# A long convolution with an expert block behind it, on one core: both transposes of a token tile in one place, half of a product on another engine, two loads exchanged, and two stages spread over more chunks

## The chip, the cores and the metric

The kernel runs on one core of a Trainium2 chip. A core has TensorE (PE in the profile; its weight loads are shown apart as PEld), VectorE (DVE), ScalarE (ACT), GpSimd (POOL) and SyncE (SP), which issues all of this kernel's DMAs. The metric is the device time of one execution in microseconds. Each engine works through its own instructions in the order in which the program has them.

## The reference

Two blocks follow each other. The first is a long convolution along the sequence, for a batch B of 4, a sequence S of 12480 and a model width D of 128:

```python
h = np.maximum(pos_emb @ w1, 0.0) @ w2          # S x D filter
h = h * np.exp(-0.01 * np.arange(S))[:, None]
u = x * v                                       # B x S x D
y = causal convolution of u with h along S      # by FFTs of length 2 S
z = x * y
```

The second takes the B * S = 49920 rows of z as tokens, with d_ff = 2048:

```python
h = z @ w_in
out = (h * np.cos(h)) @ w_out                   # 49920 x 128
```

All values are float32, two inputs (the expert's weights) come as float64.

## The kernel before

**The convolution.** The sequence is cut as 120 columns (n2) of 104 rows, and the transform of length 2 * 96 * 120 is done in two steps of small matrix products each way. A batch passes through four stages, each a generator that puts out a little work at a time: F1 (`f1_units`, 64 units), the first forward step; F2 (`f2_units`, 48 units), the second, whose results DVE multiplies with the filter's spectrum (L479, L481) and POOL adds (L482); I1 (`i1_units`, 64 units), the first inverse step, evicted by ACT and DVE (L494, L496); and I2 (`i2_units`, 30 groups of 4 columns), the second inverse step. A group of I2 needs a table `tm` of 312 KB, made or loaded from DRAM (`td`), and the 208 KB of x that belong to it (`xs`); DVE multiplies the matmuls' result by x in place (L518), and SP stores that as z in DRAM (`zd`). While a batch is in I2, x * v of the next batch is made beside it (`u_units`): loads of x and v, two multiplies for the two halves of each tile (L404), then sums and differences of the halves (L410). Batch 0's F1 to I1 and the filter's own transform come first, before any token work, in some 340 us.

**The expert block.** 98 token tiles of 128 rows times 4 (tile 0 has 104, the last fewer) go through 16 chunks of d_ff each. For a chunk, `moe_up` multiplies the transposed tile `at` by the chunk's weights into a PSUM bank `ph`; ACT and DVE reduce the phase (L753, L754); one chunk later `moe_act` takes the sine on ACT (L759) and the second product on DVE (L760), which is the bank's last reader. POOL makes sums and differences of two chunks (`moe_sums`, L768 to L772), and `moe_down`, seven chunks behind, adds into two PSUM accumulators (L785). Matmuls of both parts are issued as pairs of 64 output columns (`tiled`), which run side by side; transposes use all 128 columns.

**The order.** It is written out by hand, in one loop over chunks. Per chunk: `moe_down` of seven chunks before, the loads that are due, `moe_up`, `moe_act` of the chunk before, `moe_sums`, then special pieces at certain chunks c of a tile, and at the end as much of the convolution as is due. What is due is counted in `owed`: each chunk adds 1, and each piece that a generator puts out takes off its price, a stage's STEPS (in chunks per unit) over the parts of a unit:

```python
U_STEPS, F1_STEPS, F2_STEPS, I1_STEPS, I2_STEPS = 2.0, 0.8, 2.9, 0.8, 1.5
FIRST_STEPS, I2U_STEPS = 3.5, 3.0
```

FIRST_STEPS is for I2 of batch 0, I2U_STEPS for I2 of batches 1 and 2 (with x * v beside it), I2_STEPS for batch 3. `load(n)` (L977) runs the convolution on, whatever is owed, until all rows of tile n have been made; for tile n + 2 it stands at chunk 14 of tile n. Tile 24 is the first that needs rows of batch 1. When the last batch is done, only the expert block is left.

**A tile's way in and out.** `moe_load` brings its rows from DRAM into the single buffer `tile`. `moe_turn` transposes them on PE with four instructions (L136) into one bank and copies that to `at` on ACT (L742); it stands at chunk 3 of the tile before (at chunk 14 of tile 0, for tile 1). `moe_evict` adds up the accumulators on ACT and DVE (L799 to L806) into `ot`, at chunks 5 and 6 of the next tile. `moe_back` transposes `ot` back with four instructions (L136) into a bank and copies it to `tile` on ACT (L816), at chunk 8 of the next tile; `moe_store` sends it out at chunk 10.

**PSUM.** Of eight banks of 512 float32 columns, two are the accumulators, three are `ph` (pool `ps_h`: the ups, `moe_turn` and `moe_back`), and three are the convolution's (`ps_c`, names `cv`, by `bank()`; two while batch 0 is in I2). When the convolution is done, odd chunks' ups take those as well.

**Loads of a group of I2.** `before(j)` in `i2_units` runs one group ahead (two for batch 3): first the load of x (`load_pairs`, L385), then the table's (L681). `tm` has two buffers (three in batch 3), `xs` one more than that.

Of the kernel before, what the change touches and what calls it, by code (L numbers as in the profile page):

```python
# [9 lines left out]
F32 = mybir.dt.float32  # L10
# [7 lines left out]
P = 128  # L18
BANK = 512
# [14 lines left out]
def kernel(  # L34
# [46 lines left out]
    nc = tc.nc  # L81

    B, S, D = x.shape
# [3 lines left out]
    R = S // N2  # L87
# [14 lines left out]
    NFC = DFF // P  # L102
    G = BANK // D
    UA = 2
    NG = N2 // G
    NROWS = B * NG * R
    NALL = 1 + math.ceil((NROWS - R) / P)
# [8 lines left out]
    td = dram.tile([N2 // G, N1, G, 2, R], F32, name="td")  # L116
# [17 lines left out]
    def transpose(dst, src, ident):  # L134
        n = src.shape[0]
        nc.tensor.transpose(dst, src, ident[0:n, 0:n])  # L136
# [240 lines left out]
    def n2s(g):  # L377

        a = g * UA
        return [*range(a, a + UA), *range(N2 - UA - a, N2 - a)]  # L380

    def load_pairs(t, src, b, first, second):

        start = src[b, first:first + UA, :]
        nc.sync.dma_start(t[:, :, :], bass.AP(  # L385
            tensor=start.tensor, offset=start.offset,
            ap=[[N2 * D, R], [(second - first) * D, 2], [1, UA * D]]))
# [173 lines left out]

    SOME = range(2, NG, 5)
    REST = 3.0
    U_STEPS, F1_STEPS, F2_STEPS, I1_STEPS, I2_STEPS = 2.0, 0.8, 2.9, 0.8, 1.5
    FIRST_STEPS, I2U_STEPS = 3.5, 3.0

    def u_units(b, bufs, u, engine, side="left"):

# [84 lines left out]
    def make_group(pool, g, t, summed):  # L653

        for i, n2 in enumerate(n2s(g)):
            if i >= summed:
                make_t(t[:, i, :, :], n2, copies=rows_psum)
            else:
                spare = pool.tile([N1, 2, R], F32, name="spare", bufs=2)
                make_t(t[:, i, :, :], n2, spare=spare[:, :, :])  # L660
            yield
        nc.sync.dma_start(td[g, :, :, :, :], t[:, :, :, :])
# [7 lines left out]
    def i2_units(bank, b, bufs):  # L670

        with tc.tile_pool(name="back", bufs=2, side="left" if b else "right") as pool:
            ts, xss = {}, {}

            def before(j):
                ts[j] = pool.tile([N1, G, 2, R], F32, name="tm", bufs=bufs)
                xss[j] = pool.tile([R, 2, UA * D], F32, name="xs", bufs=bufs + 1)
                load_pairs(xss[j], x, b, n2s(j)[0], n2s(j)[UA])
                if b == 0 and j not in SOME:
                    return make_group(pool, j, ts[j], 1)  # L680
                nc.sync.dma_start(ts[j][:, :, :, :], td[j, :, :, :, :])  # L681

            def mm(j, ps, i):
                if i == 0:
                    ps = bank()
                i2_mm(ps, ts[j], j, i)
                return ps

            yield from units(NG, I2_STEPS, before, mm,
                             lambda j, ps: i2_out(pool, ps, xss.pop(j), b, j),  # L690
                             4 if b == 0 else 2, ahead=bufs - 1, skip=int(b == 0))

    def inverse_units(bank, b):

        if b + 1 == B:
            yield from i2_units(bank, b, 3)
            return
        new = u_units(b + 1, 3, slots[0:R, :, :, :],  # L700
                      lambda j, half: nc.gpsimd,
                      side="right" if b else "left")
        parts = 4 if b == 0 else 2
        for i, steps in enumerate(i2_units(bank, b, 2)):
            if i > 2 * parts:
                for _ in range(i % parts > 0 if b == 0 else 1 + i % 2):
                    next(new, None)
            yield steps * (FIRST_STEPS if b == 0 else I2U_STEPS) / I2_STEPS
        yield from new
# [16 lines left out]
    def rows_of(n):  # L726
        return first_row(n + 1) - first_row(n)
# [7 lines left out]
    def moe_turn(pool, n):  # L735
        m = rows_of(n)
        zb = zbs.pop(n)
        pt = ps_h.tile([P, BANK], F32, name="ph")
        for i in range(G):
            transpose(pt[:, i * m:(i + 1) * m], zb[0:m, i, :], ident)  # L740
        at = pool.tile([D, BANK], F32, name="at")
        nc.scalar.copy(out=at[:, 0:G * m], in_=pt[:, 0:G * m])  # L742
        ats[n] = at
# [65 lines left out]
    def moe_back(pool, n, ot):  # L809
        m = rows_of(n)  # L810
        pt = ps_h.tile([P, BANK], F32, name="ph")
        places = pt[:, :].rearrange("p (h i e d) -> p h e i d", h=2, e=2, d=CB)
        for i, block in enumerate((1, 2, 3, 0)):
            transpose(places[0:m, i // 2, i % 2], ot[:, block, 0:m], ident)
        ob = pool.tile([P, G, D], F32, name="tile", bufs=1)
        nc.scalar.copy(out=ob[0:m, :, :].rearrange("p g d -> p (g d)"), in_=pt[0:m, :])  # L816
        return ob
# [15 lines left out]
    with tc.manual_schedule():  # L833
        with tc.tile_pool(name="psum", bufs=8, space=PSUM) as psum, \
                ExitStack() as first:
            def bank():
                return psum.tile([P, BANK], F32, name="ps")
# [109 lines left out]
        ps_h = ctx.enter_context(tc.tile_pool(name="ps_h", bufs=3, space=PSUM))  # L947
# [9 lines left out]
        mpool = ctx.enter_context(tc.tile_pool(name="moe", bufs=2))  # L957
# [19 lines left out]
        def load(n):  # L977
            while made[0] * R < first_row(n + 1):
                next(conv)
            moe_load(mpool, n)  # L980
# [5 lines left out]
        hidden, pairs, gates, ots, obs = {}, {}, {}, {}, {}  # L986
        for i in range(len(steps) + LAG):
            if i >= LAG:
                pn, pc = steps[i - LAG]
                moe_down(pn, pc // 2, pc % 2, *gates[i - LAG - pc % 2])  # L990
                if pc >= NFC - 2:
                    ots[pn] = moe_evict(mpool, pn, pc % 2, ots.get(pn))
            if i < len(steps):
                n, c = steps[i]
                if n == 0 and c == NFC // 2:
                    load(1)
                if c == (NFC - 2 if n else NFC - 1) and n + 2 < NALL:
                    load(n + 2)
                if c % 2 == 0:
                    pairs[i] = mpool.tile([P, 2, BANK], F32, name="gt", bufs=4)  # L1000
                hidden[i] = moe_up(mpool, n, c, pairs[i - c % 2])
            if 0 <= i - 1 < len(steps):
                moe_act(*hidden.pop(i - 1))
            if i - 4 in pairs:
                gates[i - 4] = moe_sums(mpool, steps[i - 4][0], pairs.pop(i - 4))
            if i < len(steps):

                if c == (3 if n else NFC - 2) and n + 1 < NALL:
                    moe_turn(mpool, n + 1)
                if c == NFC // 2 and n - 1 in ots:  # L1010
                    obs[n - 1] = moe_back(mpool, n - 1, ots.pop(n - 1))
                if c == NFC // 2 + 2 and n - 1 in obs:
                    moe_store(n - 1, obs.pop(n - 1))
            owed += 1.0
            while owed > 0.0:
                owed -= next(conv, owed)
# [30 lines left out]
```

## Time and profile before

| | us |
|---|---|
| median of three runs | 3812.39 (3808.34 to 3815.78) |
| the profiled execution, its own time | 3811.25 |
| its span | 3809.4 |
| PE busy | 3674.4 |
| DVE busy | 2915.1 |
| POOL busy | 2835.7 |
| ACT busy | 2241.1 |

The profile is of one execution. A matmul's busy time is its latency, which overlaps the next one's; how densely PE works is read from the starts of its instructions in the timeline. Idle times are those of an engine ahead of an instruction, with what ended them. By the instructions' own times, the first chunk starts some 346 us into the span; I2 of batch 0 lasts to some 572 us, then F1, F2, I1 and I2 of batch 1 (with x * v of batch 2 beside I2) to some 1416 us, of batch 2 to 2256, of batch 3 to 3018; after that the expert block is alone.

### The profile page before, as it was taken

To read this page: it belongs to the slowest core of one execution; us is meant where nothing else is said; L and a number is where in the kernel's file an instruction comes from. 1 tells how busy PE (TensorE), PEld (TensorE's weight loads), DVE (VectorE), ACT (ScalarE), POOL (GpSimd) and SP (SyncE) were. 2 spreads that over 40 slices of the span, in tenths; PEclk is the share of its full clock that TensorE was granted. 3 is DMA by queue.
4 is the path that set the end of the run, shared out by engine and by line. 5 is a ranking of instruction groups with operands and counts; after the bars stand their busy time and mean duration, and the time that the engine had idled before them with its cause. 6 is when DMAs were issued, how large, how long until landed. Compare 5 with 4: busy or idle time off the path is not lost.

```text
span 3809.4 us, 101067 instructions
## 1 busy us (share of the span) xinstructions
PE 3674.4 (96%) x40298; PEld 2553.4 (67%) x40298; DVE 2915.1 (77%) x5722; ACT 2241.1 (59%) x4660; POOL 2835.7 (74%) x3361
## 2 busy tenths in 40 slices
PE   7898999999999999999999999999999999999999
PEld 6777676666677766666677666666677666666666
DVE  8887777788877667788876667788876677777777
ACT  5756665655555446655555456655554466666666
POOL 7667996588856986688846995688744577777777
PEclk9999999999999999999999999999999999999999
DMA  5253551022202650122203540122204400000000
GB/s 165 71 178 100 162 159 34 20 77 76 70 19 81 175 149 28 29 77 74 68 13 103 173 139 13 43 73 79 59 13 128 121 23 18 24 18 24 18 21 17
DMA packets 209708, 279.58 MB, mean 73 GB/s; under 512 B 17111, under 2 KB 146535, under 8 KB 209111
## 3 DMA queue, kind: packets, MB, share of 16 engines
q1 hardware_dynamic: 209239, 273.12, 24.7%
q8 instruction: 320, 5.24, 0.6%
q14 instruction: 149, 1.22, 0.1%
HBM read 193.64 MB, written 79.42 MB: 72 GB/s over the span
## 4 chain that ended last, share of the span: by engine, by line
PE 71%; DVE 8%; POOL 4%; DMA 3%; ACT 2%; issue 2%; SPq 0%; ACTq 0%; POOLq 0%; DVEq 0%
PE ph L132 24%; PE cv L132 19%; PE accb L785 15%; PE acca L785 11%; PE ph L136 3%; DVE gt L760 3%; DVE gt L754 2%; DMA tm<-td 2%; ACT gt L753 1%; POOL ts L768 1%; DMA zd<-xs 1%; POOL slots L410 1%; POOL xt L404 1%; POOL ts L771 1%; DVE t L481 0%
## 5 line engine op out<-in xcount | busy, mean ns | idle before, releaser
L753 ACT ACTIVATE gt<-ph 128x512 int32<-128x512 f32 (+1 forms) x1341 | 799.0, 596 | 1326.6 <-PE ph L132 1267.8
L754 DVE SCALAR_TENSOR_TENSOR gt<-ph,gt 128x512 f32<-128x512 f32 (+1 forms) x1341 | 922.2, 688 | 762.2 <-ACT gt L753 751.6
L768 POOL TENSOR_TENSOR ts<-gt 128x512 f32<-128x512 f32 (+2 forms) x784 | 998.7, 1274 | 641.4 <-PE accb L785 612.4
L132 PE MATMUL ph<-at,w_in_sb 128*64 128x512 f32 (+1 forms) x5364 | 1390.0, 593 | 5.3 <-DVE gt L760 2.1
L759 ACT ACTIVATE gt<-gt 128x512 f32<-128x512 f32 (+1 forms) x1568 | 972.4, 620 | 0.9 <-DVE gt L754 0.8
L760 DVE TENSOR_TENSOR gt<-ph,gt 128x512 f32<-128x512 f32 (+1 forms) x1341 | 909.9, 679 | 0.0
L785 PE MATMUL accb<-ts,w_out_sb 128*64 128x128 f32 (+2 forms) x9408 | 651.2, 272 | 0.0
L771 POOL TENSOR_TENSOR ts<-ts,gt 128x256 f32<-128x256 f32 (+2 forms) x784 | 572.1, 730 | 61.5
L772 POOL TENSOR_TENSOR ts<-gt,ts 128x256 f32<-128x256 f32 (+2 forms) x784 | 571.2, 729 | 61.4
L785 PEld LDWEIGHTS accb<-ts,w_out_sb 128*64 128x64 f32 x9408 | 544.7, 137 | 0.0
L785 PEld LDWEIGHTS acca<-gt,w_out_sb 128*64 128x64 f32 x6272 | 392.7, 137 | 222.6 <-issue 179.5
L785 PE MATMUL acca<-gt,w_out_sb 128*64 128x128 f32 (+2 forms) x6272 | 482.3, 273 | 0.0
L785 PEld LDWEIGHTS accb<-gt,w_out_sb 128*64 128x64 f32 x3136 | 220.1, 137 | 234.4 <-issue 172.5
L482 POOL TENSOR_TENSOR slots<-slots,t 120x256 f32<-120x256 f32 x384 | 280.4, 738 | 119.3 <-DVE t L481 75.7
L132 PEld LDWEIGHTS ph<-at,w_in_sb 128*64 128x64 f32 x5364 | 344.9, 137 | 19.4 <-ACT tile L816 5.4
L132 PEld LDWEIGHTS cv<-slots,tm 96*64 96x64 f32 (+1 forms) x3840 | 243.0, 128 | 142.6 <-issue 95.1
L785 PE MATMUL accb<-gt,w_out_sb 128*64 128x128 f32 (+1 forms) x3136 | 313.6, 274 | 2.9 <-DVE ot L806 0.8
L785 PE MATMUL acca<-ts,w_out_sb 128*64 128x128 f32 (+1 forms) x3136 | 308.6, 272 | 7.4 <-POOL ts L771 7.3
L132 PE MATMUL cv<-slots,tm 96*64 96x128 f32 (+1 forms) x3840 | 280.4, 288 | 22.6 <-DMA tm<-td 15.9
L132 PE MATMUL cv<-at,w_in_sb 128*64 128x512 f32 (+1 forms) x908 | 231.2, 587 | 0.0
L132 PEld LDWEIGHTS cv<-cs,slots 120*64 120x64 f32 (+1 forms) x3072 | 170.9, 124 | 79.2 <-issue 77.2
L785 PEld LDWEIGHTS acca<-ts,w_out_sb 128*64 128x64 f32 x3136 | 201.2, 137 | 10.0 <-POOL ts L771 9.9
(145 smaller groups left out, 4117.5 us busy)
## 6 DMA issues: line engine op xcount, KB each, us to landing
h<-hd SPq DMA_DIRECT2D x144, 240.0 KB
tm<-td SPq DMA_DIRECT2D x96, 312.0 KB
xt<-in_x_dram SPq DMA_DIRECT2D x120, 208.0 KB
vt<-in_v_dram SPq DMA_DIRECT2D x120, 208.0 KB
xs<-in_x_dram SPq DMA_DIRECT2D x120, 208.0 KB
zd<-xs SPq DMA_DIRECT2D x119, 208.0 KB
tile<-zd SPq DMA_DIRECT2D x96, 256.0 KB
w<-wd SPq DMA_DIRECT2D x144, 116.2 KB
```

Source lines behind the costliest of these rows:

```text
L132: nc.tensor.matmul(dst[lo:hi], left[:, lo:hi], right, start=start, stop=stop)
L136: nc.tensor.transpose(dst, src, ident[0:n, 0:n])
L404: engine.tensor_tensor(xt[:, half, :], xt[:, half, :], vt[:, half, :], op=ALU.mult)
L482: nc.gpsimd.tensor_tensor(y[:, r], y[:, r], t[:, r], op=op)
L753: nc.scalar.activation(turns, ph[:, 0:m], AF.Identity, bias=phase)
L754: nc.vector.scalar_tensor_tensor(out=part, in0=ph[:, 0:m], scalar=phase, in1=turns, op0=ALU.add, op1=ALU.subtract)
L759: nc.scalar.activation(part, part, AF.Sin, scale=scale)
L760: nc.vector.tensor_tensor(part, ph, part, op=ALU.mult)
L768: nc.gpsimd.tensor_tensor(ts[:, 0:2, 0:half], gt[:, :, half:2 * half], gt[:, 0, 0:2 * half].rearrange("p (h n) -> p h n", h=2), op=ALU.sub ...
L771: nc.gpsimd.tensor_tensor(t[2], t[1], b11, op=ALU.add)
L772: nc.gpsimd.tensor_tensor(t[3], b21, t[2], op=ALU.subtract)
L785: nc.tensor.matmul(acc[h * CB:(h + 1) * CB, place, 0:r], w_out_sb[:, pair, weight, :], right[:, h * r:(h + 1) * r], start=(pair == 0 and i ...
```

## The change

Five places are changed.

- The price of an F2 unit goes from 2.9 to 3.4 chunks, that of a group of I2 with x * v beside it from 3.0 to 3.4.
- In `before(j)` of I2 the table's load is issued ahead of that of x, and for batches 1 to 3 there is one more `xs` buffer.
- The second half of each x * v of batches 1 to 3 is multiplied on DVE, not on POOL.
- `moe_turn` takes a bank of the convolution (`bank()`) in place of a `ph` bank.
- `moe_turn` of the next tile goes from chunk 3 to chunk 8, and it and `moe_back` of the tile before are issued one behind the other ahead of chunk 8's `moe_up`, no longer behind `moe_sums`. For tile 0 the turn stays at chunk 14, now ahead of the up.

```diff
-    U_STEPS, F1_STEPS, F2_STEPS, I1_STEPS, I2_STEPS = 2.0, 0.8, 2.9, 0.8, 1.5
-    FIRST_STEPS, I2U_STEPS = 3.5, 3.0
+    U_STEPS, F1_STEPS, F2_STEPS, I1_STEPS, I2_STEPS = 2.0, 0.8, 3.4, 0.8, 1.5
+    FIRST_STEPS, I2U_STEPS = 3.5, 3.4
...
             def before(j):
                 ts[j] = pool.tile([N1, G, 2, R], F32, name="tm", bufs=bufs)
-                xss[j] = pool.tile([R, 2, UA * D], F32, name="xs", bufs=bufs + 1)
+                xss[j] = pool.tile([R, 2, UA * D], F32, name="xs", bufs=bufs + 1 + (b > 0))
+                made_here = b == 0 and j not in SOME
+                if not made_here:
+                    nc.sync.dma_start(ts[j][:, :, :, :], td[j, :, :, :, :])
                 load_pairs(xss[j], x, b, n2s(j)[0], n2s(j)[UA])
-                if b == 0 and j not in SOME:
+                if made_here:
                     return make_group(pool, j, ts[j], 1)
-                nc.sync.dma_start(ts[j][:, :, :, :], td[j, :, :, :, :])
...
         new = u_units(b + 1, 3, slots[0:R, :, :, :],
-                      lambda j, half: nc.gpsimd,
+                      lambda j, half: nc.vector if half else nc.gpsimd,
                       side="right" if b else "left")
...
         zb = zbs.pop(n)
-        pt = ps_h.tile([P, BANK], F32, name="ph")
+        pt = bank()
         for i in range(G):
             transpose(pt[:, i * m:(i + 1) * m], zb[0:m, i, :], ident)
...
                 if c == (NFC - 2 if n else NFC - 1) and n + 2 < NALL:
                     load(n + 2)
+                if c == (NFC // 2 if n else NFC - 2) and n + 1 < NALL:
+                    moe_turn(mpool, n + 1)
+                if c == NFC // 2 and n - 1 in ots:
+                    obs[n - 1] = moe_back(mpool, n - 1, ots.pop(n - 1))
                 if c % 2 == 0:
                     pairs[i] = mpool.tile([P, 2, BANK], F32, name="gt", bufs=4)
                 hidden[i] = moe_up(mpool, n, c, pairs[i - c % 2])
...
             if i < len(steps):
-
-                if c == (3 if n else NFC - 2) and n + 1 < NALL:
-                    moe_turn(mpool, n + 1)
-                if c == NFC // 2 and n - 1 in ots:
-                    obs[n - 1] = moe_back(mpool, n - 1, ots.pop(n - 1))
                 if c == NFC // 2 + 2 and n - 1 in obs:
```

## The prediction

> **What bounds the kernel now.** The first view is the page: engine busy times and the chain that ended last.
>
> ```profile
> span 3809.4 us, 101067 instructions
> ...
> PE 3674.4 (96%) x40298; PEld 2553.4 (67%) x40298; DVE 2915.1 (77%) x5722; ACT 2241.1 (59%) x4660; POOL 2835.7 (74%) x3361
> ...
> PE 71%; DVE 8%; POOL 4%; DMA 3%; ACT 2%; issue 2%; SPq 0%; ACTq 0%; POOLq 0%; DVEq 0%
> ```
>
> TensorE bounds it, at a mean granted clock of 0.992. The change removes no matmul, so only idle time and badly spaced matmuls can be won: idle is 3809.4 - 3674.4 = 135 us, and some 52 us of that lie in the first 381 us (by the busy time of the stretches 0 to 381), which the change leaves as they are. The second view, busy time by stage, shows where the rest sits (columns: stretch, its length, then busy us and instructions of PE, PEld, DVE, ACT, POOL, the clock, DMA share and GB/s). The stages are the end with the expert block alone, a second forward transform (F2), the last inverse stage with the next batch's x * v beside it (I2), and I2 of the last batch.
>
> ```profile
> 3048.00:3714.00 666.00, 664.62 (x7114) 418.56 (x7112) 522.18 (x866) 455.16 (x842) 527.35 (x577) 1.00 0.08 21
> 749.00:1042.00 293.00, 284.06 (x2928) 177.15 (x2926) 246.03 (x495) 165.63 (x301) 251.72 (x298) 1.00 0.25 74
> 1199.00:1416.00 217.00, 209.83 (x2549) 154.32 (x2547) 136.23 (x224) 103.62 (x190) 190.85 (x236) 0.99 0.59 167
> 2876.00:3018.00 142.00, 135.48 (x1756) 105.08 (x1754) 78.81 (x130) 52.73 (x97) 60.74 (x67) 1.00 0.51 151
> ```
>
> In the end stage PE is full; in the others it lacks 7 to 9 us each. The timeline of PE in the end stage shows what a full PE still loses at a group of transposes.
>
> ```profile
> 3168.31 1.03 PE L132 MATMUL ph<-at,w_in_sb 128*64 128x512 f32 x4
> ...
> 3171.55 1.03 PE L132 MATMUL ph<-at,w_in_sb 128*64 128x512 f32 x4
> ...
> 3173.07 1.03 PE L132 MATMUL cv<-at,w_in_sb 128*64 128x512 f32 x4
> 3174.03 0.66 PE L136 MATMUL ph<-ident,tile 128*128 128x128 f32 x4
> ...
> 3175.54 0.60 PE L132 MATMUL ph<-at,w_in_sb 128*64 128x512 f32 x2
> ```
>
> Two chunks take 3171.55 - 3168.31 = 3.24 us without a group and 3175.54 - 3171.55 = 3.99 us with one: a group of four costs 0.75 us. Last, who waits, in the groups of instructions (idle time before them, and its releaser):
>
> ```profile
> L136 PE MATMUL ph<-ident,tile 128*128 128x128 f32 x384 | 62.0, 284 | 10.3 <-PE ph L132 7.9 <-DMA tile<-zd 0.2
> L136 PE MATMUL ph<-ident,ot 128*128 128x128 f32 x384 | 62.0, 284 | 19.0 <-DVE gt L760 19.0
> L132 PE MATMUL cv<-slots,tm 96*64 96x128 f32 x1920 | 277.5, 288 | 22.6 <-DMA tm<-td 15.9 <-POOL tm L306 5.6 <-DVE tm L302 0.9
> ```
>
> **The change, part by part.** All sums are against the profiled execution, 3811.25 us (span 3809.4), 1.1 us under the median of the three runs.
>
> *One group of eight instead of two of four.* It happens for tiles 1 to 96. The four weight loads of a group take 0.42 us, so 0.75 - 0.42 = 0.33 us is the price of going from 64-column matmuls to a 128-column one and back: 0.10 before the first transpose (3173.07 + 0.86, the usual step from one block of ups to the next block, is 3173.93; it starts at 3174.03), and the rest behind the last. One group saves at most that, 96 x 0.33 = 32 us, and nothing if the second four pay it again. I take 0.25, near the upper end, since the second four have the first four's shape: 24 us. The Trainium skill, TensorEngine Tiling (Array Packing), Tiling Modes, says that changing the tiling mode drains the array; with one drain (an up lasts 0.59 us and the next pair starts after 0.43 us, so 0.16) at each of the two changes saved, that alone would be 31 us.
>
> *The waits at the transposes.* 10.3 + 19.0 = 29 us of idle stand before them, because each takes one of three ph banks and so waits for the second product (L760) of a chunk only two back. The turn now takes a convolution bank, and both stand ahead of the up of chunk 8. What is late next is that up, which takes the bank of chunk 6. From the end of up 7, that bank comes free after L753 of chunk 7 (0.60), L759 of 6 (0.62, behind it on ACT) and L760 of 6 (0.68), 1.90 us, plus one or two F2 products of 0.415 on DVE: 2.3 to 2.7. PE meanwhile has some 0.35 of F2, 0.76 of down (the 12 or 16 matmuls of L785), and the eight transposes, 0.75 + 0.42 = 1.17: 2.28. So up 8 waits 0 to 0.45 us, in some 30 tiles beside F2: 0 to 13, I take 9. The two copies on ACT (0.58 each) now stand ahead of L753 of 8, but run while PE does up 8, 0.86 us; if that cover went, the next L759 is late and not PE at once. The turn's own wait is for an eviction of the convolution, which the old trace can't show; per tile it lies between 0 and 0.9 us (the longest wait before a transpose), in 73 tiles with a convolution beside them. By the nearest rows, evictions of 0.35 to 0.68 us that are issued a chunk or more before, I take 0.1: 7 us. Net 29 - 9 - 7 = +13; ends +29 and 29 - 13 - 66 = -50.
>
> *Tables ahead of x, one more x buffer.* On SP, in the last batch's I2:
>
> ```profile
> 2908.22 0.34 SPq L522 DMA_DIRECT2D zd<-xs  x1
> 2911.99 0.33 SPq L385 DMA_DIRECT2D xs<-in_x_dram  x1
> 2912.36 0.39 SPq L681 DMA_DIRECT2D tm<-td  x1
> ```
>
> and in the chain of the same stretch:
>
> ```profile
> 2908.22 3.75 DMA zd<-xs
> ...
> 2916.97 3.72 DMA tm<-td
> ```
>
> SP holds the load of x until the store of z has left its buffer (3.75 us), the tables queue behind it, and PE then waits for their landing. With a fourth (fifth) buffer and the order exchanged, the tables are issued as soon as the matmuls two or three groups back are done. In this stage 6.4 us of PE's idle is put down to the tables; all of it should go. In the two I2 stages with x * v beside them it is 4.6 and 4.4 us; there SP also stands at loads of x and v for POOL's multiply (89.8 us of SP's waiting between 1199 and 1416 us), ahead of the tables as before, so I count two thirds: 6. Together 12; lower end 4 (the last batch's wait half gone), upper 25 of the 38.7 us for which weight loads waited on these tables. Past the tables are moved one load of x per group, 0.33 us of issue and 208 KB; x is needed at the end of its group, a group's time (5 to 8 us) later than the tables.
>
> *Half of x * v on VectorE.* 90 multiplies leave POOL, 0.73 us each, 66 us. On DVE they took 0.41 to 0.95 us where the old kernel has them, in the first stage, median 0.458: 41 us over three I2 stages in which DVE is 63 to 75% busy. This stage shows two prices:
>
> ```profile
> 33.78 0.91 POOL L404 TENSOR_TENSOR xt<-xt,vt 104x256 f32<-104x256 f32 x1
> 34.48 0.50 DVE L404 TENSOR_TENSOR xt<-xt,vt 104x256 f32<-104x256 f32 x1
> 35.12 0.98 POOL L410 TENSOR_TENSOR slots<-xt 104x256 f32<-104x256 f32 x1 [0.42 <-DVE xt L404]
> ```
>
> POOL's own instruction beside it takes 0.91 to 0.98 instead of 0.73 (22 us in all, if always), and the sum behind it waits for DVE: 6.9 us over 12 multiplies, 0.58 each, up to 52 us, with the chunk's POOL sums queued behind. POOL thus gets between 66 - 22 - 52 = -8 and +44 us. The Trainium skill, GPSIMD Engine Reference, Key points, says that this engine shares its SBUF interfaces with VectorE and contends with instructions of two SBUF inputs, as this one; by that rule alone the relief would be 44. What POOL can give PE is small: idle of 7.3 us before L785 by L771, 6.9 before the first forward transform (F1) by L410. I take +3, a fifth of it, since the multiply is issued a step ahead of the sum here; ends -8 (its own delay) and +12.
>
> *Pacing.* F2 spreads over 48 x 0.5 = 24 chunks more in each of three batches, I2 over 30 x 0.4 = 12 more in two. The end stage loses chunks for it; there PE is full as well, so nothing is won but a little of F2's idle, up to 4. One thing is lost: the chunk that loads tile 24 needs the first group of batch 1, and the convolution is then some 26 I1 units behind; they go out in one block, without chunks between. I1 alone ran 64 units from 270.7 to 335.3, 1.0 us each, against 0.85 of matmul spacing beside chunks (24 matmuls in 1.27 us, 16 a unit): 26 x 0.15 = 4, up to 8. Net -1; ends -8 and +4.
>
> Sum: 24 + 13 + 12 + 3 - 1 = 51; 3811.25 - 51 = 3760.
>
> **The rivals.** (1) The transposes save nothing but waits, as the second four pay the shape again, and the waits move to up 8: 0 + 0 + 12 + 3 - 1, 3797. For it: the old trace has no group of eight. Against: the 0.10 and 0.23 us stand only at changes of shape. (2) Slower: the turn takes a convolution bank where units of F1 and I1 need a new one every 0.8 chunk, and waits behind DVE, with the units after it. It decides from (51 + 7) / 73 = 0.8 us per tile; at 1.2 us, 3811 + 30 = 3841. For it: those stages already wait for evictions, 11.4 us by L425 before F1. Against: that is 0.09 us per matmul group, and no wait before a transpose was over 0.9. (3) More: the upper ends of the first three parts, 32 + 25 + 20 + 3, 3731. (4) The change is hidden, and all stays within 0.2%, some 7.6 us, about what this kernel's measurement can tell from no change.
>
> **How the numbers follow.** Chances: forecast (3735 to 3785) 0.58; rival 1 (3785 to 3804) 0.16; rival 3 0.10; rival 4 0.04; rival 2 0.12. Faster by over 0.2%: 0.58 + 0.16 + 0.10 = 0.84; same 0.04; slower 0.12. The range leaves out rival 2, rival 4 and the far part of rival 3: 3727 to 3803.
>
> **What the new profile would show.** Right: in the end stage a tile (16 chunks) takes 16 x 1.62 + 1.17 instead of 16 x 1.62 + 1.50 us; idle before L136 falls from 29 to under 10 us, with some 9 us new before the ups by L760; tables before `cv<-slots,tm` fall from 15.9 to some 4 us; POOL's busy time falls by 45 to 66 us. Wrong: PE idle before the turn on evictions (L425, L496, L481, L518), before F1 and I1 units on their banks, or on POOL's sums beside I2; or an F2 stage that is no shorter per chunk.

## The result, and the profile after

The changed kernel takes 3749.9 us (median; 3748.6 to 3750.7) where the kernel before, measured beside it, takes 3813.6 us. The ratio is 0.9835, with a 95% interval of 0.9817 to 0.9852: 1.65% faster, 63.7 us. The forecast was 3760 us, 10 us too slow, and its range of 3727 to 3803 us holds the result. The profiled execution took 3748.55 us, its span is 3746.8 us, and its granted clock 0.994, against 0.992 before.

The page of the kernel after: span, busy time of each engine (us, share, instructions), and the chain that ended last.

```profile
span 3746.8 us, 101339 instructions
...
PE 3631.1 (97%) x40298; PEld 2592.9 (69%) x40298; DVE 2962.2 (79%) x5812; ACT 2252.4 (60%) x4660; POOL 2786.1 (74%) x3271
...
PE 79%; DVE 7%; POOL 2%; ACT 2%; issue 1%; DMA 0%; ACTq 0%; SPq 0%; POOLq 0%; DVEq 0%
```

TensorE is the bound as before; DMA has left the chain (3% before), and POOL is 49.6 us less busy, inside the forecast's 45 to 66. PE has 43 us less busy time and the span is 63 us shorter, so its idle time fell from 135 to 116 us. The busy time by stretch of the kernel after (stretch, length, then busy us and instructions of PE, PEld, DVE, ACT and POOL, the clock, DMA share, GB/s) shows where; the first three stretches are those shown for the kernel before, the fourth is its last inverse stage, which now lies later.

```profile
3048.00:3714.00 666.00, 664.69 (x7270) 432.80 (x7268) 520.77 (x865) 454.39 (x834) 522.76 (x572) 1.00 0.10 27
749.00:1042.00 293.00, 287.08 (x3004) 187.64 (x3002) 249.13 (x492) 172.79 (x315) 255.24 (x299) 1.00 0.24 68
1199.00:1416.00 217.00, 216.26 (x2650) 162.23 (x2648) 156.82 (x270) 113.83 (x208) 188.61 (x222) 1.00 0.61 167
2945.00:3075.00 130.00, 130.00 (x1726) 104.55 (x1724) 76.95 (x128) 52.07 (x96) 59.82 (x66) 1.00 0.60 166
```

PE is now full in both I2 stretches (it lacked some 7 us in each); beside F2 it still lacks 5.9 of 293 us (8.9 before). The groups of PE's instructions of the kernel after (busy us, mean ns | idle time before them and what ended it) name the waits.

```profile
L132 PE MATMUL ph<-at,w_in_sb 128*64 128x512 f32 x5400 | 1406.7, 594 | 24.7 <-ACT tile L818 17.0 <-DVE gt L762 7.1
L132 PE MATMUL cv<-slots,tm 96*64 96x128 f32 x1920 | 274.6, 287 | 7.4 <-POOL tm L306 5.6 <-DVE slots L496 0.9 <-DVE tm L302 0.9
L132 PE MATMUL cv<-c,slots 104*64 104x192 f32 x768 | 159.8, 327 | 13.0 <-DVE slots L425 9.9 <-POOL slots L410 2.3
L136 PE MATMUL cv<-ident,tile 128*128 128x128 f32 x384 | 62.7, 286 | 12.2 <-issue 5.3 <-DVE t L481 3.5 <-DVE xs L518 3.4
L136 PE MATMUL ph<-ident,ot 128*128 128x128 f32 x384 | 57.7, 273 | 0.0
```

The lines of the kernel after are two further down (L762 is the old L760, L818 the old L816). The waits for tables by DMA are gone, 15.9 to 0. The waits at the transposes fell from 29.3 to 12.2 us; 5.3 of these are "issue", waits whose end the profile ties to nothing. But a wait of 24.7 us now stands before the ups, and 17.0 us of it are ended by ScalarE's copy L818, which the forecast has nowhere. In the kernel before, the ups, F1 and the downs that wait for POOL had these lines:

```profile
L132 PE MATMUL ph<-at,w_in_sb 128*64 128x512 f32 x5268 | 1367.7, 594 | 3.5 <-ACT tile L816 1.4 <-DVE gt L760 1.0 <-ACT at L742 0.2
L132 PE MATMUL cv<-c,slots 104*64 104x192 f32 x768 | 160.9, 331 | 18.6 <-DVE slots L425 11.4 <-POOL slots L410 6.9
L785 PE MATMUL acca<-ts,w_out_sb 128*64 128x128 f32 x3072 | 302.9, 273 | 6.2 <-POOL ts L771 6.1
```

PE's clock has a part in the gain as well. Behind the first chunk, the trace of the kernel before has three stretches in which the granted clock is half of full: 3.4 us at 603, 3.4 at 1365 and 6.8 at 1443 us. Each begins within 2 us of the end of a long wait of PE (3.5, 2.0 and 2.3 us). The kernel after has none behind its first chunk. The first of these places is the start of F1 of batch 1, behind a wait for POOL's sums (L410) of 3.51 us before and 2.35 us after. The columns are those of the stretches above; the first line is of the kernel before, the second of the kernel after:

```profile
603.50:607.00 3.50, 3.50 (x23) 2.85 (x23) 0.00 (x0) 0.00 (x0) 3.34 (x5) 0.52 0.42 108
601.30:604.80 3.50, 3.34 (x36) 2.69 (x38) 0.00 (x0) 0.43 (x1) 3.34 (x5) 1.00 0.42 90
```

Half the clock for 13.7 us costs PE at most 6.8 us. Over all executions, the mean granted clock is 0.9915 for the kernel before (the 21 beside the first four experiments) and 0.9935 for the kernel after (4), which is worth up to 0.0020 x 3800 = 8 us, an estimate. The forecast has no term for the clock.

A busy PE hides badly spaced matmuls, so a second measure is used below, the *lost time* of a stage: its length by the starts of chunks (a chunk counts to the stage whose matmuls it has, or that come next), less its matmuls at one usual step for each kind in the traces (an up 214.5 ns, a down 54.6, a transpose 109, F1 81, F2 111, I1 50.8, I2 59). Only differences between kernels have a meaning, and time lost to a lower clock is in them. In us, worked out from the starts in each trace:

| kernel | F1 (3) | F2 (3) | I1 (3) | I2 with x * v (2) | last I2 | end | all, with the first I2 |
|---|---|---|---|---|---|---|---|
| before | 52.7 | 58.6 | 12.3 | 31.0 | 12.9 | 19.8 | 198.6 |
| after | 36.7 | 47.4 | 17.4 | 9.8 | 3.4 | 9.4 | 135.4 |
| transposes alone | 55.8 | 46.3 | 15.0 | 20.0 | 11.3 | 11.7 | 172.2 |
| tables alone | 53.0 | 59.3 | 12.3 | 22.9 | 3.8 | 19.6 | 182.6 |
| DVE half alone | 44.5 | 59.4 | 12.3 | 27.9 | 12.0 | 19.7 | 187.1 |
| steps alone | 46.6 | 73.5 | 15.9 | 21.1 | 10.7 | 16.4 | 195.7 |
| after, transposes undone | 39.7 | 72.8 | 16.0 | 21.1 | 4.1 | 16.2 | 181.2 |
| after, tables undone | 36.9 | 47.0 | 17.5 | 10.0 | 11.1 | 9.4 | 143.6 |
| after, DVE half undone | 45.7 | 47.3 | 17.4 | 9.1 | 3.3 | 10.0 | 144.5 |
| after, steps undone | 46.7 | 45.8 | 15.2 | 9.6 | 3.2 | 12.0 | 143.6 |
| after, turn and back a chunk apart | 39.0 | 60.9 | 20.1 | 15.1 | 4.3 | 16.3 | 170.0 |
| after, turn in a bank of the ups | 42.0 | 54.2 | 16.4 | 15.6 | 4.2 | 16.6 | 158.0 |

The total fell by 63.2 us, as much as the time. The kernel before measured 3813.4 us beside the first four experiments, 3807.5 and 3808.5 beside the other two sets, so each ratio below is to the kernel before of its own set; the totals of lost time agree with the differences of the medians to within 4 us. The changed kernel was measured beside neither of the last two sets, so where a time of theirs is compared with its 3749.9 us, some 6 us are open; the lost times are the better measure there, since in stages that an edit does not touch (the tables undone, the buffer left out) they repeat to within 0.6 us.

### The profile page after: what moved, and what is told of

Its sections match the earlier page's. It is cut to its first block, busy times and chain, and to the rows that moved or that the text cites. A ratio compares the mean times of both kernels' runs of the same rounds, so it can differ in the third digit from the quotient of the medians.

```text
span 3746.8 us, 101339 instructions
## 1 busy us (share of the span) xinstructions
PE 3631.1 (97%) x40298; PEld 2592.9 (69%) x40298; DVE 2962.2 (79%) x5812; ACT 2252.4 (60%) x4660; POOL 2786.1 (74%) x3271
## 3 DMA queue, kind: packets, MB, share of 16 engines
q14 instruction: 151, 1.23, 0.1%
## 4 chain that ended last, share of the span: by engine, by line
PE 79%; DVE 7%; POOL 2%; ACT 2%; issue 1%; DMA 0%; ACTq 0%; SPq 0%; POOLq 0%; DVEq 0%
PE ph L132 28%; PE cv L132 20%; PE accb L787 16%; PE acca L787 12%; DVE gt L762 2%; DVE gt L756 2%; PE cv L136 1%; ACT gt L755 1%; PE ph L136 1%; POOL ts L770 1%; DVE slots L431 0%; ACT tile L818 0%; POOL slots L410 0%; POOL ts L773 0%; DVE slots L433 0%
## 5 line engine op out<-in xcount | busy, mean ns | idle before, releaser
L755 ACT ACTIVATE gt<-ph 128x512 int32<-128x512 f32 (+1 forms) x1374 | 818.5, 596 | 1175.2 <-PE ph L132 1123.3
L756 DVE SCALAR_TENSOR_TENSOR gt<-ph,gt 128x512 f32<-128x512 f32 (+1 forms) x1374 | 944.3, 687 | 676.8 <-ACT gt L755 666.8
L132 PE MATMUL ph<-at,w_in_sb 128*64 128x512 f32 (+1 forms) x5496 | 1428.6, 593 | 26.6 <-ACT tile L818 17.0
L762 DVE TENSOR_TENSOR gt<-ph,gt 128x512 f32<-128x512 f32 (+1 forms) x1374 | 932.3, 679 | 0.0
L787 PEld LDWEIGHTS acca<-gt,w_out_sb 128*64 128x64 f32 x6272 | 404.5, 137 | 239.1 <-issue 200.2
L787 PEld LDWEIGHTS accb<-gt,w_out_sb 128*64 128x64 f32 x3136 | 230.1, 137 | 254.8 <-issue 198.3
L132 PEld LDWEIGHTS ph<-at,w_in_sb 128*64 128x64 f32 x5496 | 354.9, 137 | 51.3 <-ACT tile L818 22.4
L132 PEld LDWEIGHTS cv<-c,slots 104*64 104x64 f32 (+1 forms) x1536 | 118.3, 137 | 114.6 <-issue 63.6
```

What stands on the lines that cost most here:

```text
L132: nc.tensor.matmul(dst[lo:hi], left[:, lo:hi], right, start=start, stop=stop)
L755: nc.scalar.activation(turns, ph[:, 0:m], AF.Identity, bias=phase)
L756: nc.vector.scalar_tensor_tensor(out=part, in0=ph[:, 0:m], scalar=phase, in1=turns, op0=ALU.add, op1=ALU.subtract)
L762: nc.vector.tensor_tensor(part, ph, part, op=ALU.mult)
L787: nc.tensor.matmul(acc[h * CB:(h + 1) * CB, place, 0:r], w_out_sb[:, pair, weight, :], right[:, h * r:(h + 1) * r], start=(pair == 0 and i ...
```

## The experiments: each part alone

Four kernels are the kernel before with one part of the change.

**The transposes**, moved and in their new bank:

```diff
-        pt = ps_h.tile([P, BANK], F32, name="ph")
+        pt = bank()
...
+                if c == (NFC // 2 if n else NFC - 2) and n + 1 < NALL:
+                    moe_turn(mpool, n + 1)
+                if c == NFC // 2 and n - 1 in ots:
+                    obs[n - 1] = moe_back(mpool, n - 1, ots.pop(n - 1))
...
-                if c == (3 if n else NFC - 2) and n + 1 < NALL:
-                    moe_turn(mpool, n + 1)
-                if c == NFC // 2 and n - 1 in ots:
-                    obs[n - 1] = moe_back(mpool, n - 1, ots.pop(n - 1))
```

> The old kernel with the transposes alone changed: turn and back together ahead of the up of chunk 8, the turn in a convolution bank. Theory A (the prediction's terms): 24 for one change of shape less per tile and 13 for the waits, so 37 us less than the old kernel, 3776. Theory B (by the stages of the two traces): the end stage went from 0.055 to 0.037 us lost per chunk, 0.29 us per tile, 28 us over 96 tiles, and beside the convolution 5 us come on top of that, 33 us less. Rival (waits only, no shape): 13 us less. All say that idle before the transposes falls from 29 us to some 12, and that new waits stand before the up that follows.

Measured: 3790.1 us, ratio 0.9940 (0.9927 to 0.9952), 23 us faster. The groups of PE in this kernel:

```profile
L132 PE MATMUL ph<-at,w_in_sb 128*64 128x512 f32 x5268 | 1372.5, 595 | 20.5 <-ACT tile L816 14.5 <-DVE gt L760 5.6
L136 PE MATMUL cv<-ident,tile 128*128 128x128 f32 x384 | 62.8, 286 | 15.6 <-DVE t L481 6.9 <-issue 3.3 <-DVE slots L496 2.8
L136 PE MATMUL ph<-ident,ot 128*128 128x128 f32 x384 | 57.7, 273 | 0.0
```

The transposes' waits fall by 29.3 - 15.6 = 13.7 us, and the ups' rise by 20.5 - 3.5 = 17.0. As a trade of waits this part loses 3 us; what it wins is something else, the spacing of the matmuls (below).

**The tables** ahead of x, with the additional buffer:

```diff
-                xss[j] = pool.tile([R, 2, UA * D], F32, name="xs", bufs=bufs + 1)
+                xss[j] = pool.tile([R, 2, UA * D], F32, name="xs", bufs=bufs + 1 + (b > 0))
+                made_here = b == 0 and j not in SOME
+                if not made_here:
+                    nc.sync.dma_start(ts[j][:, :, :, :], td[j, :, :, :, :])
                 load_pairs(xss[j], x, b, n2s(j)[0], n2s(j)[UA])
-                if b == 0 and j not in SOME:
+                if made_here:
                     return make_group(pool, j, ts[j], 1)
-                nc.sync.dma_start(ts[j][:, :, :, :], td[j, :, :, :, :])
```

> The old kernel with only the tables asked for ahead of x and one x buffer more in batches 1 to 3. Theory A (the prediction's term): 12 us less, half of it in the last batch's I2 (6.4 us) and half in the two I2 stages with x * v beside them. Theory B: the three I2 stages lost 16, 15 and 13 us over the matmuls' own spacing before and 5, 5 and 3 after; if the tables are the larger share of that, 17 to 22 us less, with PE's idle by tables before cv<-slots,tm gone.

Measured: 3796.3 us, ratio 0.9957 (0.9945 to 0.9970), 17 us faster. The waits for tables by DMA go from 15.9 to 3.3 us, and the lost time falls by 8.1 us in the two I2 stages with x * v and by 9.1 in the last one.

```profile
L132 PE MATMUL cv<-slots,tm 96*64 96x128 f32 x1920 | 276.7, 288 | 9.8 <-POOL tm L306 5.6 <-DMA tm<-td 3.3 <-DVE tm L302 0.8
```

**Half of x * v on DVE**:

```diff
-                      lambda j, half: nc.gpsimd,
+                      lambda j, half: nc.vector if half else nc.gpsimd,
```

> The old kernel with only the second half of x * v on DVE in batches 1 to 3. Theory A (the prediction's term): 3 us less, between 8 more and 12 less. Theory B: POOL's lag behind I2 held up the first units of F1, and the three F1 stages with the few chunks ahead of them lost 16 us less after the change than before; if that is this edit's, 10 to 13 us less, and idle before F1's matmuls by L410 falls from 6.9 to some 2 us. POOL busy some 60 us less, DVE some 40 us more.

Measured: 3805.0 us, ratio 0.9978 (0.9969 to 0.9986), 8.3 us faster. Part of it is won where PE waited for GpSimd: before F1 (`cv<-c,slots` by L410) 6.9 to 3.9 us, and before the downs (`acca` by the old L771) 6.1 to 2.0.

```profile
L785 PE MATMUL acca<-ts,w_out_sb 128*64 128x128 f32 x3072 | 302.8, 273 | 2.0 <-POOL ts L771 2.0
L132 PE MATMUL cv<-c,slots 104*64 104x192 f32 x768 | 159.9, 329 | 15.6 <-DVE slots L425 11.4 <-POOL slots L410 3.9
```

Part of it goes with the clock, and the two are not separated: this trace has no stretch at half clock behind the first chunk, and the mean granted clock of its 11 executions is 0.9927 against 0.9915, worth up to 4.6 us by the same estimate. In all five traces with these multiplies on POOL alone, F1 of batch 1 begins with a wait of 3.5 us, and the clock is halved within 2 us of its end; in the nine with half of them on DVE the wait is 2.4 us, and the clock is halved there in four.

In the kernel after, the waits for GpSimd and the multiplies are these, first as it is, then (second fence) with this part undone:

```profile
L787 PE MATMUL acca<-ts,w_out_sb 128*64 128x128 f32 x3072 | 305.9, 273 | 1.1 <-POOL ts L773 1.1
L404 POOL TENSOR_TENSOR xt<-xt,vt 104x256 f32<-104x256 f32 x138 | 106.3, 775 | 20.1 <-DMA vt<-in_v_dram 18.9 <-DVE slots L425 0.9
L404 DVE TENSOR_TENSOR xt<-xt,vt 104x256 f32<-104x256 f32 x102 | 65.7, 644 | 0.2 <-DMA vt<-in_v_dram 0.2
```

```profile
L787 PE MATMUL acca<-ts,w_out_sb 128*64 128x128 f32 x3072 | 306.4, 273 | 7.1 <-POOL ts L773 7.1
L132 PE MATMUL cv<-c,slots 104*64 104x192 f32 x768 | 161.3, 329 | 18.0 <-DVE slots L425 9.9 <-POOL slots L410 7.2
L404 POOL TENSOR_TENSOR xt<-xt,vt 104x256 f32<-104x256 f32 x228 | 169.4, 752 | 19.8 <-DMA vt<-in_v_dram 19.5
L404 DVE TENSOR_TENSOR xt<-xt,vt 104x256 f32<-104x256 f32 x12 | 6.8, 569 | 0.3 <-DMA vt<-in_v_dram 0.3
```

These rows mix the first stage, which the change leaves alone, with batches 1 to 3. In batches 1 to 3 alone, the 90 multiplies on DVE take 0.66 us each in the mean (0.41 to 1.94, median 0.49), and the 90 that stay on POOL 0.751 instead of 0.733. The Trainium skill, GPSIMD Engine Reference, Key points, speaks of contention between GpSimd and DVE instructions with two SBUF inputs; these times fit one that is large for some of DVE's multiplies and small for POOL's, 90 x 0.018 = 2 us in all.

**The steps**:

```diff
-    U_STEPS, F1_STEPS, F2_STEPS, I1_STEPS, I2_STEPS = 2.0, 0.8, 2.9, 0.8, 1.5
-    FIRST_STEPS, I2U_STEPS = 3.5, 3.0
+    U_STEPS, F1_STEPS, F2_STEPS, I1_STEPS, I2_STEPS = 2.0, 0.8, 3.4, 0.8, 1.5
+    FIRST_STEPS, I2U_STEPS = 3.5, 3.4
```

> The old kernel with only the prices of an F2 unit (2.9 to 3.4) and of an I2 group with x * v (3.0 to 3.4). Theory A (the prediction's term): 1 us more, between 8 more and 4 less, with one block of some 26 I1 units at chunk 365. Theory B: the longer groups of I2 give tables and POOL more time, and hide what the other edits also take away; then it is 5 to 10 us less alone, and the four edits alone add up to more than the whole change.

Measured: 3812.4 us, ratio 0.9997 (0.9988 to 1.0006): no difference. The table of lost time shows that this is a balance, not an absence: the I2 stages win 12 us, F1 6, the end 3, and the F2 stages lose 15 and the I1 stages 4. Of the gains, 3.4 us are the clock's in this trace (6.8 us at half clock behind the first chunk instead of 13.7). The groups say why F2 loses, and that the waits for tables fall from 15.9 to 5.6 us:

```profile
L136 PE MATMUL ph<-ident,tile 128*128 128x128 f32 x384 | 61.8, 283 | 16.1 <-PE ph L132 11.2 <-DVE t L481 1.4 <-DVE gt L760 0.6
L136 PE MATMUL ph<-ident,ot 128*128 128x128 f32 x384 | 61.7, 283 | 23.1 <-DVE gt L760 22.8
L132 PE MATMUL cv<-slots,tm 96*64 96x128 f32 x1920 | 277.6, 288 | 13.1 <-POOL tm L306 5.6 <-DMA tm<-td 5.6 <-DVE slots L496 0.9
```

The waits at the transposes rise from 29.3 to 39.2 us. An F2 stage now takes in 165 chunks instead of 141, so 10 or 11 tiles instead of 8 or 9; in that of batch 2, the steps from an up to a group of transposes lose 17.0 us over 21 groups instead of 12.3 over 17, 4.7 of the stage's 6.3.

## The experiments: the change with one part undone

The four parts alone sum to 23.3 + 17.1 + 8.3 + 0.9 = 49.6 us, and the whole gives 63.7. So four kernels are the changed kernel with one of the diffs above taken back.

> The changed kernel with the transposes as they were: the turn at the fourth chunk and the back at the ninth, both after their up, and the turn in the bank of the ups. Theory of plain addition (each part is worth in the whole what it is worth alone): 3750 + 23 = 3773 us. Theory of interplay (what more spread work costs is paid at the transposes, and the change of the transposes is what makes the other parts pay fully): 3781 to 3788 us, 31 to 38 above the changed kernel, with the waits ahead of the turn and the back together above 25 us as in the run of the pacing alone (39 us there) and the loss of a stage with its second branch at 18 us or more instead of 15.5 to 16.

> The changed kernel with the tables asked for after x and without the additional buffer of x. Addition: 3750 + 17 = 3767 us. Interplay: 3758 to 3762 us, since the run of the pacing alone had already cut the wait for tables from 15.9 to 5.6 us, so that only the last inverse stage (9 us in the run of the tables alone) is left to them.

> The changed kernel with all of x * v on GpSimd. Addition: 3750 + 8 = 3758 us. Interplay: 3750 to 3753 us, if the time that GpSimd's queue cost was the wait of the back's neighbours and is now covered; 3765 us or more if the denser inverse stage after the pacing needs GpSimd more than before.

> The changed kernel with the two old step counts. Addition: 3750 + 1 = 3751 us (the steps alone measured 3812.4 against 3813.4). Interplay: 3760 to 3765 us, since the parts alone sum to 49.7 us and the whole gives 63.6: the spread work gains some 16 us in the inverse stages in either kernel, and lost as much at the transposes of the second-branch stages only where these still waited.

| undone | time, us | ratio to before | above the changed kernel, us | the part alone, us |
|---|---|---|---|---|
| transposes | 3794.4 | 0.9964 (0.9951 to 0.9976) | 44.5 | 23 |
| tables | 3757.2 | 0.9867 (0.9854 to 0.9881) | 7.3 | 17 |
| DVE half | 3758.8 | 0.9870 (0.9857 to 0.9884) | 9.0 | 8 |
| steps | 3757.9 | 0.9870 (0.9855 to 0.9886) | 8.0 | 1 |

The DVE half adds: 8.3 us alone, 9.0 in the whole, of which some 4 may be the clock's (a mean granted clock of 0.9925 with it undone, 0.9935 in the changed kernel). The transposes are worth twice as much in the whole, more than either expectation gave them. The kernel with them undone shows the waits that they take away there:

```profile
L136 PE MATMUL ph<-ident,tile 128*128 128x128 f32 x384 | 61.7, 283 | 17.3 <-PE ph L132 13.2 <-DVE gt L762 1.4 <-DVE t L481 0.4
L136 PE MATMUL ph<-ident,ot 128*128 128x128 f32 x384 | 61.6, 283 | 25.0 <-DVE gt L762 24.8
```

The old places would wait 42.3 us in the new schedule, not 29.3, and F2 would lose 72.8 us instead of 47.4. That is the loss that the steps alone had; with the transposes moved, the steps cost F2 only 47.4 - 45.8 = 1.6 us, not 15. The tables are worth less in the whole, because the steps had already taken most of the wait of the two earlier I2 stages: with the tables undone these lose 10.0 us as against 9.8, and only the last stage goes back, from 3.4 to 11.1. There the waits for tables stand again (us in total, times, longest):

```profile
PE cv L132 <- DMA tm<-td: 5.2, 5, 2.3
```

With the steps undone, the F1 stages lose 10.0 us more and the end 2.6, while I1 and F2 lose 3.8 less. The waits before F1 by L425 and L410 explain 4.7 of the 10.0 (13.1 + 3.8 instead of 9.9 + 2.3 us), and the clock 1.7 (3.4 us at half clock at 601 us, in the kernel after none); what the other 3.6 are was not found. The mean granted clock is 0.9925 here too.

## The experiments: what the transposes gain by

**A chunk apart.** The changed kernel, with the back one chunk after the turn; places ahead of an up and banks stay.

```diff
-                if c == NFC // 2 and n - 1 in ots:
+                if c == NFC // 2 + 1 and n - 1 in ots:
                     obs[n - 1] = moe_back(mpool, n - 1, ots.pop(n - 1))
```

> The changed kernel with the back one chunk later than the turn (both still ahead of an up, same pools): two groups of four transposes a tile instead of one of eight. Theory that a change of shape has a price of its own: 96 tiles x 0.25 to 0.29 us = 24 to 28 us, seen in the end stage too, where no up waits for a copy; with nine more ups that take the back's bank (32 instead of 23, 0.7 us each, 6 us) 3774 to 3784 us. Rival, that only waits were removed: 3750 to 3757 us, and the end stage unchanged.

Measured: 3784.0 us, ratio 0.9931 (0.9918 to 0.9943), 34 us above the changed kernel. Of its groups, the ups:

```profile
L132 PE MATMUL ph<-at,w_in_sb 128*64 128x512 f32 x5400 | 1407.2, 596 | 30.1 <-ACT tile L818 23.2 <-DVE gt L762 6.7
```

Waits by L818 are 23.2 - 17.0 = 6.2 us more. In the end stage, where PE waits for next to nothing either way, the 20 tiles up to chunk 1500 lose 17.7 instead of 11.7 us (the table's last part has the final chunks too): 0.30 us for the second group of a tile. For 96 tiles that is 28.8, and 28.8 + 6.2 = 35.0 us against 34.6 of lost time. So a group of transposes has a price of its own, and one group less is nearly half of what the whole change gains. The changes between ups and downs, all of 64 columns, have none: the 3.24 us of two plain chunks are their usual steps, 8 x 0.2145 + 28 x 0.0546 us. The price thus stands where 64 and 128 columns meet; that it is the change of shape, and nothing else that a group of transposes brings, was not tested apart. The timeline of PE in the kernel after (start, duration, instruction), at a tile in the end stage, shows the group of eight:

```profile
3176.91 1.03 PE L132 MATMUL ph<-at,w_in_sb 128*64 128x512 f32 x4
...
3178.43 1.03 PE L132 MATMUL cv<-at,w_in_sb 128*64 128x512 f32 x4
3179.51 0.44 PE L787 MATMUL accb<-gt,w_out_sb 128*64 128x128 f32 x4
...
3180.54 0.66 PE L136 MATMUL cv<-ident,tile 128*128 128x128 f32 x4
3181.03 0.60 PE L136 MATMUL ph<-ident,ot 128*128 128x128 f32 x4
3181.56 1.08 PE L132 MATMUL ph<-at,w_in_sb 128*64 128x512 f32 x4
...
3183.12 1.03 PE L132 MATMUL cv<-at,w_in_sb 128*64 128x512 f32 x4
```

From the up of chunk 7 to that of chunk 9 it is 3183.12 - 3178.43 = 4.69 us, 1.45 more than the 3.24 of two plain chunks. Of these, 0.22 are no part of the group: the down behind the up of chunk 7, which opens a new accumulator, starts 1.08 us after it and not 0.86, and did so in the old kernel too. The group of eight costs 1.23 us, and inside it the second four follow the first without a loss, at the transposes' usual step. In the old timeline the turn's four cost 0.75, as shown before, and the back's 0.76 (2.28 us from the up of chunk 8, at 3182.28, to the next, against 1.52 for such a step without a group).

**The turn in a bank of the ups**, as before the change, in its new place.

```diff
-        pt = bank()
+        pt = ps_h.tile([P, BANK], F32, name="ph")
```

> The changed kernel with the turn in the bank ring of the ups, as before the change; the place of the transposes stays. By the banks as allotted, the back takes the turn's own bank in 39 of 96 tiles, all beside the convolution, and must wait there for ScalarE's copy of it (0.6 to 0.8 us: 23 to 31 us), while the ups that took the back's bank (17 us) fall from 23 to 1. Theory that the bank matters by these waits: 3750 + 27 - 17 = 3760 us (3755 to 3766), end stage unchanged. Rival, that the conv bank costs the convolution's evictions the 7 us that the prediction charged: 3743 to 3750 us.

Measured: 3770.9 us, ratio 0.9899 (0.9885 to 0.9912), 21 us above the changed kernel, more than expected.

```profile
L132 PE MATMUL ph<-at,w_in_sb 128*64 128x512 f32 x5400 | 1402.7, 594 | 13.0 <-ACT at L744 9.3 <-DVE gt L762 1.9 <-ACT tile L818 0.7
L136 PE MATMUL ph<-ident,tile 128*128 128x128 f32 x384 | 63.0, 287 | 0.2
L136 PE MATMUL ph<-ident,ot 128*128 128x128 f32 x384 | 60.4, 280 | 31.8 <-ACT at L744 26.3 <-DVE gt L762 5.4
```

The expected exchange is there: 26.3 us, 39 times, before the back for the copy of the turn out of the same bank, and 0.7 instead of 17.0 before the ups by L818. Missed was that the next up often takes the turn's bank and waits for that copy as well (9.3 us), and that this reaches the end stage: there an up starts 0.49 us after the last transpose instead of 0.20, 6 us in 20 tiles. So the bank counts, by the same kind of wait.

**The two calls swapped**, back ahead of turn, to hide the copy L818 behind the turn.

```diff
+                if c == NFC // 2 and n - 1 in ots:
+                    obs[n - 1] = moe_back(mpool, n - 1, ots.pop(n - 1))
                 if c == (NFC // 2 if n else NFC - 2) and n + 1 < NALL:
                     moe_turn(mpool, n + 1)
-                if c == NFC // 2 and n - 1 in ots:
-                    obs[n - 1] = moe_back(mpool, n - 1, ots.pop(n - 1))
```

> The changed kernel with the two calls swapped: the back ahead of the turn, so that the copy L818 runs beside the turn's four transposes (0.5 us) before the up that takes the back's bank. If the new wait of the ups is that copy: 17 us falls to some 6, 3738 to 3742 us. Rival, that the back now stands where it waits for VectorE (the release of its bank, which the turn had covered): 3746 to 3752 us, with a new idle time ahead of L136 of 8 us or more.

Measured: 3747.7 us, ratio 0.9838 (0.9824 to 0.9851): the same as the changed kernel. Its waits at the transposes fall from 12.2 to 3.8 us, so the rival's new wait is not there, but the ups' wait by L818 does not fall either: 20.1 us, 28 times 0.72. Its line among PE's waits (us in total, times, longest), and the timeline at one tile beside F2:

```profile
PE ph L132 <- ACT tile L818: 20.1, 28, 0.7
```

```profile
873.46 0.66 PE L136 MATMUL ph<-ident,ot 128*128 128x128 f32 x4
...
873.96 0.60 PE L136 MATMUL cv<-ident,tile 128*128 128x128 f32 x4
...
874.64 0.59 ACT L818 COPY tile<-ph 128x512 f32<-128x512 f32 x1 [0.87 <-ACT gt L761]
875.12 0.59 ACT L744 COPY at<-cv 128x512 f32<-128x512 f32 x1
...
875.28 1.08 PE L132 MATMUL ph<-at,w_in_sb 128*64 128x512 f32 x4 [0.72 <-ACT tile L818]
```

The four transposes of the back are through by 874.12, and the copy starts at 874.64, 0.08 us after the last of the turn's (874.56). By the events in the trace PE signals ACT only there. The program says why: `tile` is one buffer for both ways. The turn reads it, the copy L818 writes it, so the copy has to wait for the turn wherever it is put. A second buffer of `tile` was not tried.

**The order of the loads without the additional buffer.**

```diff
-                xss[j] = pool.tile([R, 2, UA * D], F32, name="xs", bufs=bufs + 1 + (b > 0))
+                xss[j] = pool.tile([R, 2, UA * D], F32, name="xs", bufs=bufs + 1)
```

> The changed kernel without the additional buffer of x: only the order of the two loads. If the order does it: 3749 to 3752 us. If the buffer does it: 3756 to 3759 us, as with both parts undone (3757.2 us), with the loss in the last inverse stage alone (3.4 us to 11).

Measured: 3751.2 us, ratio 0.9847 (0.9833 to 0.9860), and 136.3 us of lost time against 135.4. The last I2 stage loses 3.3 us, as in the changed kernel. The order does it; beside the new order, the buffer does nothing that can be measured. The buffer with the old order was not run.

No kernel here beats the changed one by more than the measurement can tell.

## Why the prediction was right, and where it was not

The sum was 51 us, the result 63.7; by their values in the whole, four of five terms had the right sign.

- **One group of eight: 24 us taken, 28.8 shown.** The size of 0.25 us per tile was cut from a reading of 0.33; the end stage shows 0.30. The forecast for a tile there, 16 x 1.62 + 1.17, came out with 1.23 for the group (beside the 0.22 of the new accumulator, which it had left out on both sides). The Trainium skill's rule that a change of tiling mode drains the array (TensorEngine Tiling (Array Packing), Tiling Modes), which the prediction worked out as an estimate of 31 us, is nearer than the 24. Rival 1, that the second four pay again, is refuted by the kernel with the groups a chunk apart and by the steps inside the group of eight.
- **The waits: +13 taken, -3 alone, +10 in the whole.** The step that failed is "that up, which takes the bank of chunk 6". In 23 of 73 tiles beside the convolution the up takes the bank that the back has just used (by the banks as the program allots them; the trace has 23 such waits), and waits 0.74 us for ScalarE's copy L818: 17.0 us. The two copies had been said to "run while PE does up 8"; for these tiles up 8 waits for one of them. What the step did count, L762 before the ups, was put at 9 and is 7.1. The turn's waits (put at 7, all on evictions of the convolution) are 12.2, of which 6.9 are ended by L481 and L518 and 5.3 by nothing that the profile shows. In the whole the term pays, because the old places would have waited 42 us there and not 29 (transposes undone: 42.3 + 4.5 us at transposes and ups; with them, 12.2 + 24.7).
- **Tables: 12 taken, 17 alone, 7 in the whole.** The last stage's part, 6, measured 8 to 9. The 6 for the earlier stages measured 8 alone and nothing in the whole, since the wider steps cover these loads too; the prediction had no such overlap. The buffer, counted as part of this, does nothing beside the new order.
- **DVE half: 3 taken, 8.3 alone, 9.0 in the whole.** The step that failed is "a fifth of it". PE's two waits for GpSimd, 7.3 and 6.9 us as quoted, fell by 7.1 us in the part alone, a half, and in the whole to 2.3 each: 9.6 of 14.2, two thirds. A second step is missing: the clock, which was halved less often beside the shorter waits, up to some 4 us of this part by the estimate above. POOL's wait for DVE's product before its sum, priced at up to 52 us, rose by 2.6 (6.9 to 9.5). The 0.458 us for the multiply on DVE fits the median (0.49) but not the mean (0.66), which cost nothing visible.
- **Steps: -1 taken, +1 alone, +8 in the whole.** Alone it is right by a balance that it did not see: the I2 stages gain 12 us, and the F2 stages lose 15 as long as the transposes stand behind an up. The block of I1 units in one go, put at 4 us, is small: the one chunk of the kernel after that holds it, 400 I1 matmuls in 26.8 us, loses 1.9 us, and the first I1 stage 5.2 instead of 4.2. Up to some 4 of the 8 us in the whole are the clock's by the estimate, for which the sum has nothing here either.

So the miss of 13 us is not one term. Shape +5, DVE half +6 and steps +9 were too low, tables -5 and waits -3 too high, by their values in the whole: 51 + 12 = 63. The sum over those values, 28.8 + 10 + 7.3 + 9 + 8 = 63, meets the measured 63.7; but undoing the transposes costs 44.5, not 38.8, so some 6 us of that part are not placed in a wait or in the price of a group. That the total came within 10 us is thus partly luck: errors of 3 to 9 us in all five terms, of both signs. Rival 2, waits of the turn in the ring of conv banks, is there at a seventh of its price: 12.2 us, 0.17 for each of the 73 tiles, where it decides from 0.8 and was priced at 1.2. (Its 0.09 us per matmul group is too high in any case: 11.4 us over the 192 F1 units are 0.06.) Rival 3, the upper ends, asked for 80 us; its sum takes 20 for the waits, whose own upper end was stated as 29. Rival 4, no change, is out.

## What to carry to other kernels

Where two short runs of another matmul shape interrupt a full TensorE, put them into one place first, and look at waits second: the spacing was worth 29 us here, the trade of waits 3 to lose or 10 to win, depending on the rest of the schedule. After a wait of some 2 us or more of an otherwise full TensorE, look at the clock column too: here, where a wait shrank from 3.5 to 2.4 us, less time at half clock stood beside it (3.4 or 6.8 us in five traces, none or 3.4 in nine). Before a block is moved ahead of another, list every buffer that it shares with its neighbours, SBUF as well as PSUM, and whose copy frees it; the bank that is handed out next may be the one just filled. Parts of a change that ease the same wait do not add, and parts of which one removes the other's cost add to more: test with one part undone, and not only with one part alone.

## What the runs showed that was not expected

Spreading work wider gained nothing alone and 8 us in the whole, mainly because it took more tiles into a stage where each tile's transposes waited. And the price of one more group of transposes, 0.30 us, is the same whether the group follows an up (before) or a down (a chunk apart): in the end stage a tile loses 0.88 us with two groups (21.2 us over 387 chunks, 17.7 over 320) and 0.585 with one.
